# Listing one PSUM eviction further ahead in the hand-written order of a fused attention and feed-forward kernel

## Chip, cores and metric

The kernel runs on one core of a Trainium2 chip. The metric is the device time of one execution in microseconds (us). The kernel before took 239.92 us (median of 3 runs, 239.82 to 240.09).

## What is computed

Eight batches with eight heads, 576 tokens of 64 elements each, go through an attention without a score matrix: q gets a softmax over its 64 elements, k a softmax over the 576 tokens, and then k is multiplied with v first. The result, as 4608 rows of 512, goes through a gated feed-forward block with four weight matrices.

```python
def _attn_ref(q, k, v):                        # 8 x 8 x 576 x 64 each
    q_s = np.exp(q - max over the last axis);   q_s /= sum over the last axis + 1e-9
    k_s = np.exp(k - max over axis 2);          k_s /= sum over axis 2 + 1e-9
    kv = np.einsum('bhsd,bhse->bhde', k_s, v)
    return np.einsum('bhsd,bhde->bhse', q_s, kv)

def _moe_ref(x, w1, w2, w3, w_out):             # x 4608 x 512; 512x1024 twice, 1024x1024, 1024x512
    a = x @ w1
    b = x @ w2
    h = a * b @ w3
    return h @ w_out
```

(The four lines of the softmaxes are written shorter here than in the source.)

## The kernel before

The two weights behind the product are folded into one at the start (W3O = w3 times w_out). After that each batch b goes through an attention part and gives 576 rows of x. Of these, 512 are chunk b of the feed-forward block; the 64 that are left, the tail, are gathered over all eight batches in one tile xtail, and that is chunk 8, worked last. Everything that TensorE multiplies is in 16 bits.

The work is cut into named steps, and a step is written with its parts joined by points. Those that matter here:

- kmx.b, cba.b, cbx.b, cb.b, ksub.b, kexp.b: the maximum of k over the tokens. kmx (VectorE, line 501, two halves for later batches) reduces within the partitions, cba (VectorE) is a transposition of 32 x 32 blocks (line 517) and a reduction (line 520), cbx four small copies on ScalarE (line 528), cb one more reduction and transposition on VectorE (lines 534 and 536). ksub (line 578) subtracts it on GpSimd, and kexp is the exponential on ScalarE.
- kv.b: k times v on TensorE (line 603). kve.b adds the epsilon on ScalarE (line 620), and kv2.b divides on VectorE (lines 631 and 633).
- qn.b.p, qd.b.p: the last multiplication of q's softmax (GpSimd, line 677) and its transposition by a DMA on SP's queue (line 700).
- xm.b.h and xt.b: q times kv on TensorE (line 725), xm for the 512 rows of the chunk in two halves of two PSUM banks each, xt for the 64 rows of the tail, in two banks with 128 columns used. xs.b.h.i and xts.b.i scale them out of PSUM (ScalarE: line 339, VectorE: line 341), the first into x of the chunk, the second into xtail.
- up.1.c.s.u and up.0.c.s.u: chunk c times w2 and times w1 (line 857), four matmuls into one bank each. bs.c.s.u moves the first out of PSUM (line 335) on ScalarE or VectorE, and ab.c.s.u multiplies the second with it on VectorE (line 872).
- down.c.t: eight matmuls with W3O (line 879). os.c.t moves the result out (line 335), and st.c.t stores it by SP's queue (line 905).

PSUM is divided into pools: pab with four banks for the up products (and, from batch 3 on, for xt and half of xm), po with two banks for down (and for the other half of xm), att with two for the rest. A step that takes a bank waits until the step that empties it is done.

The order of the work is written out by hand: the long string ORDER lists all 793 steps, PICKS says which engine works each eviction and each elementwise step, and `Plan.run` emits the steps one after another in that order. Each engine works its own instructions in the order in which they were emitted; between engines there are only semaphores for data and for buffers. So the place of a step in ORDER decides what is in front of it on its own engine, and nothing else. An exception are steps added with the port flag: among the first 580 steps, `link` adds a wait between such steps when they change from GpSimd to VectorE or back. The evictions xs and xts carry no such flag, ksub, qsub and qn do.

xts.4.1 is the eviction of the second of the two banks of xt.4, the tail of chunk 4; PICKS gives it to VectorE. It stands in line 116 of the kernel before, behind cba.6 of the same engine. Behind it come down.3.1, down.3.2, kv2.5 and then up.1.4.0.0, the first product of chunk 4, which takes one of the pab banks. In line 833 the two xts steps are added:

```python
for i in range(2):
    A(("xts", b, i), moves(128), 0,
      lambda eng, i=i: xs(("xt", b), i, lambda: xtail[:, i::2, b * HALF:(b + 1) * HALF], eng),
      [("xt", b)], gives=[("xt", b)])
```

Of the kernel before, what the change touches and what calls it, by code (L numbers as in the profile page):

```python
# [17 lines left out]
class Plan:  # L18
# [93 lines left out]
os.2.1 down.2.2 down.2.3 cb.5 ksub.5.0 bs.3.0.5 qd.4.0 ab.3.0.5 qrc.5.1 ab.3.0.4 up.1.3.0.6  # L112
up.0.3.0.6 kv2.4 os.2.2 os.2.3 qmx.6.1 bs.3.0.6 xm.4.1 xt.3 qeps.5.0 ab.3.0.6 qrc.5.0 xs.4.1.1
ksub.5.1 kexp.5.0 qn.5.0 xs.4.1.0 qmx.6.0 k.6 up.1.3.0.7 bs.3.0.7 up.0.3.0.7 ab.3.0.7 down.3.0
kmx.6.0 os.3.0 kmx.6.1 kexp.5.1 xts.3.0 xts.3.1 xm.4.0 xt.4 kv.5 kve.5 xs.4.0.0 xts.4.0 xs.4.0.1
qn.5.1 cba.6 xts.4.1 down.3.1 down.3.2 kv2.5 up.1.4.0.0 vc.6.0 bs.4.0.0 cbx.6 st.2.2 up.0.4.0.0
up.1.4.0.1 up.0.4.0.1 up.1.4.0.2 qd.5.0 st.2.1 qd.5.1 st.2.3 ab.4.0.0 qsub.6.1 bs.4.0.1 st.3.0 q.7
k.7 v.7 os.3.1 os.3.2 st.3.1 ab.4.0.1 cb.6 xm.5.1 xm.5.0 bs.4.0.2 xs.5.0.1 xs.5.0.0 xs.5.1.1
qexp.6.1 ksub.6.1 up.0.4.0.2 up.1.4.0.3 qsub.6.0 ab.4.0.2 up.0.4.0.3 up.1.4.0.4 bs.4.0.3 up.0.4.0.4
# [881 lines left out]
```

## Time and profile before

| | |
|---|---|
| median of 3 runs | 239.92 us |
| the profiled execution | 240.03 us |
| its span, first to last instruction | 238.2 us |
| mean granted TensorE clock | 0.999 |
| TensorE busy (matmul) | 229.9 us, 97% of the span |
| VectorE busy | 172.9 us, 73% |
| ScalarE busy | 122.0 us, 51% |
| GpSimd busy | 115.5 us, 48% |
| moved by DMA | 46.84 MB, 197 GB/s over the span |

In the profile PE is TensorE, PEld its weight loads, DVE is VectorE, ACT is ScalarE, POOL is GpSimd and SPq the queue of SyncE, which issues most of the transfers. Times are microseconds from the start of the span. A row of the timeline gives the start, the time taken, the engine, the line of the kernel, the operation and its operands with the number of instructions that were merged, and in brackets the idle time in front of it with what ended it. A row of the waits gives the engine and line that waited, for what, the total, the number of times and the longest. Buffer numbers are left out of names, so xt, xm and the up products all appear as pab or po.

### The profile page before, as it was taken

Reading aid. Unit: us, or ns where it says so; the run is one execution under the profiler, and the core shown is the slowest. Engines: PE = TensorE matmul, PEld = TensorE weight load, DVE = VectorE, ACT = ScalarE, POOL = GpSimd, SP = SyncE. Lnnn points to the kernel's source line nnn. Section 1 sums busy time; section 2 is a strip of 40 time slices with the busy share of each in tenths; the row PEclk is TensorE's granted clock in tenths of the full one; section 3 lists DMA queues with packets and bytes.
Section 4 is the critical chain, followed back from the end, with each engine's and each line's share of the span. In section 5 each row is a group of like instructions: output and inputs, shape, how many; then the busy total and the mean of one; then the engine's idle time right before and its main releaser. Section 6 shows DMA issues by size and latency. Waiting matters only on the chain.

```text
span 238.2 us, 4852 instructions
## 1 busy us (share of the span) xinstructions
PE 229.9 (97%) x1935; PEld 119.2 (50%) x1935; DVE 172.9 (73%) x263; ACT 122.0 (51%) x225; POOL 115.5 (48%) x75
## 2 busy tenths in 40 slices
PE   7698999999999999999999999999999999999994
PEld 2445658865857444444443444444544444444443
DVE  2758699989889998999997799589554443444430
ACT  1442766498757867798754856574315011103021
POOL 8467168679939998596980938340500000000000
PEclk9999999999999999999999999999999999999999
DMA  6999999999999999998688945640630005144253
GB/s 208 214 307 209 342 202 303 321 306 385 296 218 300 402 359 273 390 384 151 237 115 210 398 153 101 132 89 3 106 84 0 0 4 131 25 96 94 53 132 132
DMA packets 40038, 46.84 MB, mean 197 GB/s; under 512 B 18384, under 2 KB 24272, under 8 KB 40016
## 3 DMA queue, kind: packets, MB, share of 16 engines
q1 hardware_dynamic: 32480, 34.81, 52.0%
q0 software_dynamic: 7536, 11.73, 21.2%
q8 instruction: 15, 0.25, 0.4%
q14 instruction: 7, 0.06, 0.1%
HBM read 38.80 MB, written 9.44 MB: 202 GB/s over the span
## 4 chain that ended last, share of the span: by engine, by line
PE 86%; DMA 6%; DVE 5%; POOL 1%; issue 1%; ACT 0%; DVEq 0%; ACTq 0%; POOLq 0%
PE pab L857 52%; PE po L879 21%; DMA k<-in_k_dram 6%; PE po L469 4%; PE po L894 3%; PE pkv L603 2%; DVE km L501 2%; PE xm L725 1%; PE w3t L457 1%; PE pab L725 1%; DVE ab L872 1%; DVE kmx L510 1%; PE po L725 0%; POOL wosb L416 0%; POOL w L416 0%
## 5 line engine op out<-in xcount | busy, mean ns | idle before, releaser
L872 DVE TENSOR_TENSOR ab<-pab,bsb 128x512 f16<-128x512 f32 x72 | 48.4, 682 | 30.5 <-PE pab L857 15.8
L857 PE MATMUL pab<-x,w2sb 128*128 128x512 f16 (+1 forms) x320 | 66.0, 337 | 0.6 <-DVE xtail L341 0.6
L857 PE MATMUL pab<-x,w1sb 128*128 128x512 f16 (+1 forms) x320 | 65.9, 337 | 0.0
L879 PE MATMUL po<-W3O,ab 128*128 128x512 f16 x256 | 59.2, 379 | 0.0
L857 PEld LDWEIGHTS <-w1sb 128*128 128x128 f16 x352 | 34.1, 98 | 28.4 <-issue 0.8
L857 PEld LDWEIGHTS <-w2sb 128*128 128x128 f16 x352 | 33.5, 98 | 29.0 <-DVE xtail L341 1.1
L335 ACT CAST bsb<-pab 128x512 f16<-128x512 f32 x47 | 27.1, 585 | 27.8 <-PE pab L857 27.4
L578 POOL TENSOR_TENSOR k<-k,cb 128x1152 f32<-128x1152 f32 x12 | 31.5, 2632 | 20.2 <-issue 10.8
L677 POOL TENSOR_TENSOR en<-eq,qr 128x1280 f16<-128x1280 f16 (+1 forms) x15 | 32.8, 2193 | 17.0 <-ACT qr L664 10.0
L879 PEld LDWEIGHTS <-ab 128*128 128x128 f16 x256 | 24.5, 98 | 29.0 <-issue 0.4
L335 ACT COPY osb<-po 128x512 f32<-128x512 f32 (+1 forms) x26 | 14.8, 575 | 40.9 <-PE po L879 35.4
L645 POOL TENSOR_TENSOR q<-q,qm 128x1024 f32<-128x1024 f32 (+1 forms) x14 | 29.7, 2124 | 5.8 <-issue 4.1
L640 DVE TENSOR_REDUCE qm<-q 128x16 f32<-128x1024 f32 (+1 forms) x16 | 21.4, 1340 | 3.5 <-DMA q<-in_q_dram 3.5
L658 DVE TENSOR_REDUCE qr<-eq 128x20 f32<-128x1280 f16 (+1 forms) x16 | 21.4, 1336 | 1.7 <-ACT eq L653 1.7
L335 DVE CAST bsb<-pab 128x512 f16<-128x512 f32 x25 | 17.1, 683 | 7.5 <-PE pab L857 6.9
L586 ACT ACTIVATE ek<-k 128x1152 f16<-128x1152 f32 x16 | 18.6, 1163 | 6.8 <-DVE k L578 3.6
L653 ACT ACTIVATE eq<-q 128x1024 f16<-128x1024 f32 (+1 forms) x16 | 18.5, 1163 | 3.9 <-DVE q L645 3.0
L501 DVE TENSOR_REDUCE km<-k 128x128 f32<-128x1152 f32 x8 | 17.3, 2166 | 0.0
L469 PE MATMUL po<-wosb,w3T 128*128 128x512 f16 x64 | 15.5, 379 | 0.7 <-DMA wosb<-in_moe_w_out_dram 0.5
L335 DVE COPY osb<-po 128x512 f32<-128x512 f32 (+1 forms) x11 | 7.2, 664 | 5.9 <-PE po L894 5.6
L335 ACT CAST v<-v 128x1152 f16<-128x1152 f32 x9 | 10.3, 1159 | 1.9 <-DMA v<-in_v_dram 1.9
L469 PEld LDWEIGHTS <-w3T 128*128 128x128 f16 x64 | 5.8, 98 | 7.3 <-issue 1.0
(78 smaller groups left out, 190.7 us busy)
## 6 DMA issues: line engine op xcount, KB each, us to landing
out_dram<-osb SPq DMA_DIRECT2D x64, 128.0 KB, 2.4
q<-in_q_dram SPq DMA_DIRECT2D x6, 1152.0 KB, 7.9
v<-in_v_dram SPq DMA_DIRECT2D x5, 1152.0 KB, 9.1
k<-in_k_dram SPq DMA_DIRECT2D x4, 1152.0 KB, 8.8
k<-in_k_dram POOLq DMA_DIRECT2D x3, 1152.0 KB, 13.6
v<-in_v_dram POOLq DMA_DIRECT2D x1, 1152.0 KB, 12.0
k<-in_k_dram SPq DMA_DIRECT2D x2, 576.0 KB, 7.6
v<-in_v_dram SPq DMA_DIRECT2D x2, 576.0 KB, 9.5
```

Of the source, the lines that this page charges most:

```text
L335: return [(nc.scalar.copy if eng == "ACT" else engine[eng].tensor_copy)(out=out, in_=in_)]
L469: nc.tensor.matmul(st["pf", ft], lhsT=st["w3T", ft][:, gt, :], rhs=wosb[:, gt, :], start=(gt == 0), stop=(gt == N_FT - 1))
L501: dve.tensor_reduce(out=st["km", b][:, two(hp), :], in_=kb[:, two(hp), :, :].rearrange("p h j d -> p h d j"), axis=AX.X, op=ALU.max)
L578: return [engine[eng].tensor_tensor(out=kb[:, two(hp), :, :], in0=kb[:, two(hp), :, :], in1=st["cb", b][:, two(hp), None, :].broadcast_to( ...
L586: nc.scalar.activation(out=st["ek", b][:, hp, :, :].rearrange("p j (i d) -> p i j d", i=2), in_=kb[:, two(hp), :, :], func=AF.Exp)
L640: dve.tensor_reduce(out=st["qm", b][:, :, j], in_=qb[:, :, j, :], axis=AX.X, op=ALU.max)
L645: return [engine[eng].tensor_tensor(out=qb[:, :, j, :], in0=qb[:, :, j, :], in1=st["qm", b][:, :, j, None].broadcast_to([P, HH, n, D]), op ...
L658: dve.tensor_reduce(out=st["qr", b][:, :, slice(*PARTS[p])], in_=st["eq", b, p], axis=AX.X, op=ALU.add)
L677: return [engine[eng].tensor_tensor(out=st["en", b][:, j, :, :].rearrange("p j h d -> p h j d"), in0=st["eq", b, p], in1=st["qr", b][:, :, ...
L857: nc.tensor.matmul(st["p", one, c, sub, u][:, a * (t1 - t0):(a + 1) * (t1 - t0)], lhsT=w[:, ct, fb * P:(fb + 1) * P], rhs=x()[:, ct, t0:t1 ...
L872: dve.tensor_tensor(out=st["ab", c][:, nf * u:nf * u + nf, t0:t1], in0=cut(st["p", 0, c, sub, u]), in1=cut(st["bsb", c, sub, u]), op=ALU.mult)
L879: nc.tensor.matmul(st["po", c, tb], lhsT=st["ab", c][:, ft, tb * P:(tb + 1) * P], rhs=W3O[:, ft, :], start=(ft == 0), stop=(ft == N_FT - 1))
```

## The change

The name xts.4.1 moves in ORDER from behind cba.6 to directly behind xt.4, the step whose result it takes out of PSUM. The seven steps between (kv.5, kve.5, xs.4.0.0, xts.4.0, xs.4.0.1, qn.5.1 and cba.6) are listed after it instead, in the order that they had. The engine stays VectorE; in PICKS only the place of the entry changes.

```diff
@@ -112,8 +112,8 @@
-kmx.6.0 os.3.0 kmx.6.1 kexp.5.1 xts.3.0 xts.3.1 xm.4.0 xt.4 kv.5 kve.5 xs.4.0.0 xts.4.0 xs.4.0.1
-qn.5.1 cba.6 xts.4.1 down.3.1 down.3.2 kv2.5 up.1.4.0.0 vc.6.0 bs.4.0.0 cbx.6 st.2.2 up.0.4.0.0
+kmx.6.0 os.3.0 kmx.6.1 kexp.5.1 xts.3.0 xts.3.1 xm.4.0 xt.4 xts.4.1 kv.5 kve.5 xs.4.0.0 xts.4.0
+xs.4.0.1 qn.5.1 cba.6 down.3.1 down.3.2 kv2.5 up.1.4.0.0 vc.6.0 bs.4.0.0 cbx.6 st.2.2 up.0.4.0.0
```

4 rows, old and new, of the table PICKS are left out of this document.

## The prediction

> **What bounds the kernel now.** I read the page first: busy time by engine, the shares of the chain that ended last, and the groups of instructions with the idle time in front of them.
>
> ```profile
> span 238.2 us, 4852 instructions
> ...
> PE 229.9 (97%) x1935; PEld 119.2 (50%) x1935; DVE 172.9 (73%) x263; ACT 122.0 (51%) x225; POOL 115.5 (48%) x75
> ...
> PE 86%; DMA 6%; DVE 5%; POOL 1%; issue 1%; ACT 0%; DVEq 0%; ACTq 0%; POOLq 0%
> ...
> L857 PE MATMUL pab<-x,w2sb 128*128 128x512 f16 (+1 forms) x320 | 66.0, 337 | 0.6 <-DVE xtail L341 0.6
> ```
>
> TensorE is busy for 97% of the span and carries 86% of the last chain, so the kernel is paced by TensorE, and what can be won is the time in which it stands still. The last row names one such place: a matmul of the first product stood 0.6 us behind an eviction into xtail on VectorE. The view of TensorE's waits lists all of them:
>
> ```profile
> PE w3t L457 <- DMA w<-in_moe_w_dram: 2.4, 3, 1.3
> PE po L362 <- DVE zero L357: 1.6, 1, 1.6
> PE pab L857 <- DVE xtail L341: 0.6, 1, 0.6
> PE po L469 <- DMA wosb<-in_moe_w_out_dram: 0.5, 1, 0.5
> PE po L469 <- DVE w3T L335: 0.2, 1, 0.2
> ```
>
> Four of the five rows belong to the weights and constants at the start. Only the third lies inside the pipeline, and it is the step that the change moves. The chain of waits shows it too: the eviction ends it on VectorE, and from 125.62 it runs on TensorE up to the last eviction (the pieces left out are all TensorE's until 235.25).
>
> ```profile
> 124.95 0.42 DVE mx L520
> 125.37 0.21 DVE xtail L341
> 125.58 0.05 issue
> 125.62 4.49 PE pab L857 x20
> ...
> 235.31 0.32 ACT osb L335
> ```
>
> **The stall in detail.** Here is the timeline around it, VectorE first, then TensorE and its weight loads (PEld), then ScalarE.
>
> ```profile
> 122.25 2.19 DVE L501 TENSOR_REDUCE km<-k 128x128 f32<-128x1152 f32 x1
> 124.47 0.45 DVE L517 STREAM_TRANSPOSE kmq<-km 128x256 f32<-128x256 f32 x1
> 124.95 0.42 DVE L520 TENSOR_REDUCE mx<-kmq 128x8 f32<-128x256 f32 x1
> 125.28 0.28 DVE L341 TENSOR_SCALAR xtail<-pab 128x128 f16<-128x128 f32 x1
> 125.48 0.17 DVE L631 RECIPROCAL rc<-rc 128x4 f32<-128x4 f32 x1
> ...
> 120.34 0.47 PE L725 MATMUL pab<-qT,kv 64*64 64x512 f16 x12
> 124.18 0.81 PE L879 MATMUL po<-W3O,ab 128*128 128x512 f16 x3
> 125.62 0.55 PEld L857 LDWEIGHTS <-w2sb 128*128 128x128 f16 x4 [1.13 <-DVE xtail L341]
> 125.62 1.04 PE L857 MATMUL pab<-x,w2sb 128*128 128x512 f16 x4 [0.64 <-DVE xtail L341]
> 126.50 1.03 PE L857 MATMUL pab<-x,w1sb 128*128 128x512 f16 x4
> 127.36 1.03 PE L857 MATMUL pab<-x,w2sb 128*128 128x512 f16 x4
> ...
> 122.55 0.62 ACT L339 ACTIVATE x<-pab 128x512 f16<-128x512 f32 x1
> ...
> L879 PE MATMUL po<-W3O,ab x18: 379/379/389, 119.8 to 124.6; 128*128 128x512 f16 x18
> ```
>
> The waiting instruction is the first weight load of up.1.4.0.0. Its PSUM bank is the one that xt.4 filled for its second half, and xts.4.1 must empty it first. The three L879 rows end at 124.18 + 0.81 = 124.99; one matmul takes 0.379, so the last of them started at 124.61, which is the 124.6 of the last row. Between 126.50 and 127.36 lie four matmuls, so they start 0.215 apart when nothing holds them, though each is shown for 0.379. The next matmul could have started at 124.61 + 0.215 = 124.82 and started at 125.62. **The stall is therefore 0.80 us**, not the 0.64 that the row prints, which counts from the modelled end of the matmul before.
>
> **The change part by part.** On VectorE xts.4.1 passes two instructions, the transposition of 0.45 and the reduction of 0.42 (both are cba.6). The other steps that it passes, kv.5 on TensorE, kve.5, xs.4.0.0, xts.4.0 and xs.4.0.1 on ScalarE, and qn.5.1 on GpSimd, lie on other engines, whose built orders stay as they were. It issues no transfer and passes no step of SP's queue, and it takes no part in the hand-made chain between VectorE and GpSimd, since its step is added without the port flag. The bank that up.1.4.0.0 takes stays the same, and its weight load still waits for xts.4.1, now at a VectorE count that is lower by two.
>
> Its input has long been there: xt.4's matmuls are among the twelve L725 rows and ended by 120.34 + 0.47 = 120.81. So it starts as soon as the reduction before it lets go. That reduction ends at 122.25 + 2.19 = 124.44. In the old order xts.4.1 started at 125.28, while the reduction in front of it is shown to 124.95 + 0.42 = 125.37, an overlap of 0.09. The pair below shows as much behind the very kind of reduction that it will now follow:
>
> ```profile
> 146.40 2.09 DVE L501 TENSOR_REDUCE km<-k 128x128 f32<-128x1152 f32 x1
> 148.40 0.68 DVE L872 TENSOR_TENSOR ab<-pab,bsb 128x512 f16<-128x512 f32 x1
> ```
>
> The reduction there ends at 148.49, the next one starts at 148.40, so 0.09. I take a start at 124.44 - 0.09 = 124.35, an end at 124.35 + 0.28 = 124.63, and a release after the same 0.06 as before (125.28 + 0.28 = 125.56 against 125.62): the weight load can go at 124.69. The weight load itself takes 0.098:
>
> ```profile
> L857 PEld LDWEIGHTS <-w2sb 128*128 128x128 f16 x352 | 33.5, 98 | 29.0 <-DVE xtail L341 1.1
> ```
>
> So the matmul is ready at 124.79, and TensorE itself is free at 124.82. The stall goes whole: **-0.80 us**, from 125.62 to 124.82, and no more than that, since the matmul before is then the limit. Only 0.03 is to spare: each 0.1 by which the eviction comes later than 124.35 costs some 0.07 to 0.1 of the gain.
>
> [...]
>
> What else could hold that first matmul? It reads the x of chunk 4, whose last part ScalarE wrote at 122.55 + 0.62 = 123.17, well ahead of 124.82. Nothing else is late there.
>
> The two instructions of cba.6 go back by at most 0.28. Who needs them is ScalarE's four small copies, and behind those cb.6 and GpSimd's subtraction:
>
> ```profile
> 126.70 0.58 ACT L335 CAST bsb<-pab 128x512 f16<-128x512 f32 x1 [2.49 <-PE pab L857]
> 127.31 0.82 ACT L528 COPY mx<-mx 32x8 f32<-32x8 f32 x4
> 130.80 2.63 POOL L578 TENSOR_TENSOR k<-k,cb 128x1152 f32<-128x1152 f32 x1 [6.45 <-issue]
> ```
>
> The copies stand behind bs.4.0.0, which itself waits for TensorE; with TensorE 0.80 earlier they come at 126.51, and cba.6 ends at 125.37 + 0.28 = 125.65 at the latest. A cover of 0.86 remains, so I cost this at nothing. The reciprocal and kv2.5 behind do not move, as the three instructions ahead of them keep their sum.
>
> **Does 0.80 reach the end?** From 125.62 on no row of TensorE's waits is left, so it arrives by its own pace; what matters is whether what it meets there is late by then. The nearest meeting is xm.5.1, which needs the two po banks that os.3.1 and os.3.2 empty; a later one is ScalarE's cast of v.7, which waits for a transfer that does not move.
>
> ```profile
> 127.63 0.69 DVE L872 TENSOR_TENSOR ab<-pab,bsb 128x512 f16<-128x512 f32 x1 [1.39 <-PE pab L857]
> 128.24 1.28 DVE L335 COPY osb<-po 128x512 f32<-128x512 f32 x2
> 130.04 0.41 PE L725 MATMUL po<-qT,kv 64*64 64x512 f16 x4
> ...
> 139.93 1.16 ACT L335 CAST v<-v 128x1152 f16<-128x1152 f32 x1
> 142.90 0.59 ACT L335 COPY osb<-po 128x512 f32<-128x512 f32 x1 [1.81 <-PE po L879]
> ```
>
> The two copies end at 128.24 + 1.28 = 129.52, and xm.5.1 would now come at 130.04 - 0.80 = 129.24. But the copies follow ab.4.0.0, which had stood idle 1.39 for TensorE, so they move ahead by 0.80 as well, to 128.72. The cast of v.7 cannot start earlier than its data; ScalarE then idles 1.81 for TensorE, so 0.80 less still leaves 1.01. VectorE, GpSimd and ScalarE in between are released by TensorE's chunk 4 products in the same way, and move with it.
>
> **The sum.** The profiled execution took 240.03 (span 238.2 and 1.83 around it); 240.03 - 0.80 = 239.23. It lies 0.11 above the median of the runs, 239.92, so as a median I forecast **239.12**, or 0.33% less. A measurement of this kernel can tell about 0.2%, or 0.48, from no change: the borders are 239.44 and 240.40.
>
> **The rivals.** [...] Against it are the two overlaps; 6%. (2) TensorE gains 0.80 and meets the po banks not yet empty, since os.3.1 and os.3.2 are held by their output buffers or something else that does not move. If they end at 129.52 as before, xm.5.1's second bank is free at 129.58, 0.34 after its new time; 0.46 is left, a median of 239.46. For it speaks that of TensorE's meetings this is the closest that I see; against it the idle 1.39 before ab.4.0.0. 10%. (3) Slower: the k chain. cba.6 ends 0.28 later, and if ScalarE's copies, cb.6 and GpSimd's subtraction at 130.80 pass that on, the exponentials and bs casts behind them on ScalarE come 0.28 later, then VectorE, and TensorE waits. The copies also stand in front of bs.4.0.1 and bs.4.0.2 on ScalarE. That decides from the point where the slip outlasts the cover of 0.86; a slip of 0.28 does not, unless the copies have to wait for something else of cba.6. If all 0.28 passed and nothing of the gain were left, 239.92 + 0.28 = 240.20; if it held up both evictions one after the other, 239.92 + 0.56 = 240.48. 4%, half for each. (4) The change does nothing: the pool hands up.1.4.0.0 a bank that is freed as late as before, or VectorE's order stays. The built order speaks against it; 239.92, 3%.
>
> **How the numbers follow.** The forecast keeps 77%. The range runs from 238.92 (0.80 gained, and 0.2 for the runs, which lay from 239.82 to 240.09) to 239.60, which takes in the first two rivals with 0.14 above the second; it holds nine in ten by these cases, and I leave some of that for what I have not seen. Faster by over 0.2% are the forecast and the first rival, 83%; within 0.2% are the second, the fourth and half of the third, 15%; slower by over 0.2%, 2%.
>
> **What would show it.** In the profile after: xts.4.1 at about 124.35 in front of the transposition; no row of TensorE's waits with xtail; the first L857 matmul of chunk 4 at about 124.82; and every later TensorE row, xm.5.1 at 129.24 for one, 0.80 earlier, up to a span of 237.4. The forecast is wrong if the L857 row still waits after 124.9, or if a new wait stands in front of xm.5.1 or later.

## The result: 239.31 us against 239.93

The changed kernel took 239.31 us (median of 21 runs, 238.97 to 239.71), the kernel before 239.93 on the same chip (21 runs, 239.77 to 240.14): a ratio of 0.9975, with a 95% interval of 0.9968 to 0.9982. It is faster by 0.62, or 0.26%. The profiled execution after took 239.15, with a span of 237.4; the profiled execution before had 240.03 and 238.2.

First the page of the kernel after: the span, the busy times, the shares of the chain that ended last, and the group of first products, whose last column is the idle time in front of it. Then all of TensorE's waits.

```profile
span 237.4 us, 4852 instructions
...
PE 229.5 (97%) x1935; PEld 119.1 (50%) x1935; DVE 172.7 (73%) x263; ACT 122.1 (51%) x225; POOL 115.5 (49%) x75
...
PE 90%; DMA 6%; DVE 1%; POOL 1%; issue 1%; ACT 0%; ACTq 0%; DVEq 0%; POOLq 0%
...
L857 PE MATMUL pab<-x,w2sb 128*128 128x512 f16 (+1 forms) x320 | 66.0, 337 | 0.0
```

```profile
PE w3t L457 <- DMA w<-in_moe_w_dram: 2.5, 3, 1.4
PE po L362 <- DVE zero L357: 1.6, 1, 1.6
PE po L469 <- DMA wosb<-in_moe_w_out_dram: 0.5, 1, 0.5
PE po L469 <- DVE w3T L335: 0.2, 1, 0.2
```

The idle time in front of the first products went from 0.6 to 0.0. The wait for xtail is gone, the four others are those of the start, and no new one has come. VectorE's share of the last chain fell from 5% to 1%: the chain used to lead back from the stalled product into VectorE, and now stays on TensorE. TensorE's own busy time is about as before (229.5 against 229.9), as it should be: no work was taken away.

The timeline of the kernel after around the place, VectorE first, then TensorE with its weight loads, then ScalarE:

```profile
122.21 2.18 DVE L501 TENSOR_REDUCE km<-k 128x128 f32<-128x1152 f32 x1
124.30 0.29 DVE L341 TENSOR_SCALAR xtail<-pab 128x128 f16<-128x128 f32 x1
124.49 0.44 DVE L517 STREAM_TRANSPOSE kmq<-km 128x256 f32<-128x256 f32 x1
124.97 0.42 DVE L520 TENSOR_REDUCE mx<-kmq 128x8 f32<-128x256 f32 x1
125.31 0.17 DVE L631 RECIPROCAL rc<-rc 128x4 f32<-128x4 f32 x1
...
121.31 3.63 PE L879 MATMUL po<-W3O,ab 128*128 128x512 f16 x16
124.64 0.67 PEld L857 LDWEIGHTS <-w2sb 128*128 128x128 f16 x4 [0.19 <-DVE xtail L341]
124.78 1.03 PE L857 MATMUL pab<-x,w2sb 128*128 128x512 f16 x4
129.19 0.41 PE L725 MATMUL po<-qT,kv 64*64 64x512 f16 x4
...
126.45 0.82 ACT L528 COPY mx<-mx 32x8 f32<-32x8 f32 x4
```

The eviction into xtail now stands between the long reduction and the transposition, and its shown time overlaps both: it starts 0.09 ahead of the reduction's end, and the transposition starts 0.10 ahead of the eviction's (124.49 against 124.30 + 0.29 = 124.59). So it puts the transposition off by little: 124.49 against 124.47, in an execution that is 0.05 ahead here. The first weight load of chunk 4 still waits for it, by 0.19, but the matmul does not: its row has no bracket, and it starts at 124.78, one interval behind the last matmul of down.3.2. Followed matmul by matmul through the two traces, every start from 73.3 (xm.2.0) up to the last matmul of down.3.2 lies 0.05 earlier than before, and every start from the first product of chunk 4 to the end of the kernel lies 0.84 to 0.86 earlier. The step between the two, 0.80, is the stall. Ahead of 73.3 the two executions differ by other amounts, from the weights at the start on, so the 0.05 is a difference between executions and not of the change.

### The profile page after: what moved, and what is told of

Its sections match the earlier page's. It is cut to its first block, busy times and chain, and to the rows that moved or that the text cites. A ratio compares the mean times of both kernels' runs of the same rounds, so it can differ in the third digit from the quotient of the medians.

```text
span 237.4 us, 4852 instructions
## 1 busy us (share of the span) xinstructions
PE 229.5 (97%) x1935; PEld 119.1 (50%) x1935; DVE 172.7 (73%) x263; ACT 122.1 (51%) x225; POOL 115.5 (49%) x75
## 4 chain that ended last, share of the span: by engine, by line
PE 90%; DMA 6%; DVE 1%; POOL 1%; issue 1%; ACT 0%; ACTq 0%; DVEq 0%; POOLq 0%
PE pab L857 53%; PE po L879 24%; DMA k<-in_k_dram 6%; PE po L469 4%; PE po L894 3%; PE pkv L603 2%; PE xm L725 1%; PE pab L725 1%; PE w3t L457 1%; PE po L725 1%; DVE kmx L510 1%; POOL wosb L416 0%; POOL w L416 0%; DVE kmx L511 0%; DVE w3T L335 0%
```

## The experiments

Two theories stood against one another. **A, the release:** the first product of chunk 4 waits for its PSUM bank; what counts is only when that bank is emptied, and by which engine does not matter. **B, VectorE's sequence:** what counts is the order and the length of VectorE's own work at this place, and the bank only shows it. A variant of A, called A1 below, adds that executions differ from one another only in what lies ahead of chunk 4, and that the old stall absorbed late arrivals of TensorE; A2, against it, has a wait behind 125 that holds up some executions.

For each run I took two numbers from its trace, matmul by matmul: the start of the last matmul of down.3.2 (the arrival) and that of the first product of chunk 4. The stall is their difference less 0.2155, the spacing of matmuls that nothing holds up. The last column is the time from that first product to the end of the last matmul.

| run | arrival | first product | stall | from there to the end |
|---|---|---|---|---|
| before | 124.609 | 125.623 | 0.80 | 109.61 |
| after | 124.563 | 124.779 | 0.00 | 109.60 |
| e1_half | 124.696 | 125.217 | 0.31 | 109.61 |
| e2_late | 124.728 | 124.944 | 0.00 | 109.60 |
| e3_act | 124.776 | 124.992 | 0.00 | 109.60 |
| e4_again (the change) | 124.599 | 124.814 | 0.00 | 109.60 |
| e5_dummy_after | 124.821 | 125.037 | 0.00 | 109.60 |
| e6_dummy_before | 125.067 | 125.283 | 0.00 | 109.60 |
| e7_third (the change) | 124.759 | 124.975 | 0.00 | 109.60 |
| e8_fourth (the change) | 124.799 | 125.015 | 0.00 | 109.60 |
| e9_store_after | 124.530 | 124.746 | 0.00 | 109.60 |
| e10_store_before | 124.531 | 125.546 | 0.80 | 109.61 |
| e11_after_side (the change) | 124.738 | 124.954 | 0.00 | 109.60 |
| e12_store_side | 124.592 | 124.808 | 0.00 | 109.60 |

**e1_half: half of the move.** cba.6 is split (cbr.6 is its reduction, line 520), and xts.4.1 stands between its two instructions.

```diff
-qn.5.1 cba.6 xts.4.1 down.3.1 down.3.2 kv2.5 up.1.4.0.0 vc.6.0 bs.4.0.0 cbx.6 st.2.2 up.0.4.0.0
+qn.5.1 cba.6 xts.4.1 cbr.6 down.3.1 down.3.2 kv2.5 up.1.4.0.0 vc.6.0 bs.4.0.0 cbx.6 st.2.2 up.0.4.0.0
```

> xts.4.1 stands between the two instructions of cba.6, behind the transposition and ahead of the reduction. Theory A (the gain is the earlier release of the PSUM bank, and nothing else): the eviction starts about 0.09 ahead of the transposition's end, at 124.84, and ends at 125.12, TensorE starts chunk 4 at about 125.18 instead of 125.62; the stall shrinks from 0.80 to 0.36, so 0.44 us faster than before, some 239.5, and slower than the whole change. Theory B (the gain comes from VectorE's own sequence, in which the eviction fills a gap between two dependent instructions, so that kv2.5 comes 0.17 us earlier): the gap is filled here too, so as fast as the whole change, 239.3.

It took 239.78 (11 runs) against 240.07 of the kernel before (20 runs), a ratio of 0.9985 (0.9976 to 0.9994). VectorE, the weight load and TensorE in its timeline:

```profile
124.54 0.45 DVE L517 STREAM_TRANSPOSE kmq<-km 128x256 f32<-128x256 f32 x1
124.91 0.25 DVE L341 TENSOR_SCALAR xtail<-pab 128x128 f16<-128x128 f32 x1
125.08 0.40 DVE L520 TENSOR_REDUCE mx<-kmq 128x8 f32<-128x256 f32 x1
125.21 0.55 PEld L857 LDWEIGHTS <-w2sb 128*128 128x128 f16 x4 [0.63 <-DVE xtail L341]
125.22 1.04 PE L857 MATMUL pab<-x,w2sb 128*128 128x512 f16 x4
```

The release comes at 124.91 + 0.25 = 125.16, the weight load 0.05 later and the product with it. A part of the stall is left, 0.31, so 0.49 of 0.80 is won in the trace; the medians show 0.29, and the interval (0.14 to 0.58) holds both. The stall follows the moment of release, as A has it; B, which expected the time of the whole change, missed.

**e2_late: the eviction even later than before.** It is moved in the other direction, behind kv2.5.

```diff
-qn.5.1 cba.6 xts.4.1 down.3.1 down.3.2 kv2.5 up.1.4.0.0 vc.6.0 bs.4.0.0 cbx.6 st.2.2 up.0.4.0.0
+qn.5.1 cba.6 down.3.1 down.3.2 kv2.5 xts.4.1 up.1.4.0.0 vc.6.0 bs.4.0.0 cbx.6 st.2.2 up.0.4.0.0
```

> xts.4.1 stands behind kv2.5 on VectorE, later than in the kernel before by the reciprocal and the two multiplications. Theory A: the eviction starts at about 125.88, TensorE's first weight load of chunk 4 goes at 126.22, 0.60 later than before, a stall of 1.40; 0.60 slower than before if the end of the kernel follows TensorE one to one, some 240.5. Theory B: VectorE's sequence is as long as before, and kv2.5 even comes 0.2 earlier, so the same time as before or a little faster, 239.7 to 239.9.

A was wrong here, and so was B: 239.25 (6 runs), a ratio of 0.9969 (0.9957 to 0.9980), as good as the change itself, where A expected 240.5 and B 239.7 to 239.9.

```profile
121.48 3.63 PE L879 MATMUL po<-W3O,ab 128*128 128x512 f16 x16
124.73 0.75 PEld L857 LDWEIGHTS <-w2sb 128*128 128x128 f16 x4
124.94 1.03 PE L857 MATMUL pab<-x,w2sb 128*128 128x512 f16 x4
126.06 0.28 DVE L341 TENSOR_SCALAR xtail<-pab 128x128 f16<-128x128 f32 x1
```

The eviction starts at 126.06, over a microsecond behind the product that used to wait for it. The built programs tell why: the pool handed the products other banks.

| kernel | banks of the first four products of chunk 4 (3 is the bank that xts.4.1 empties) |
|---|---|
| before, after, e1_half | 3, 1, 2, 0 |
| e2_late, e6_dummy_before | 1, 2, 3, 0 |
| e3_act | 1, 2, 0, 3 |

In e2_late the first product takes bank 1, which ScalarE empties with x of chunk 4 by 122.64 (its eviction starts at 122.04 and takes 0.60), and bank 3 goes to the third product. The traces agree: in e2_late and e6_dummy_before the third product, and no longer the first, carries the wait for VectorE's semaphore; its first weight load goes at 126.46 in e2_late, behind the eviction's end at 126.06 + 0.28 = 126.34, and at 126.80 in e6_dummy_before, behind 126.26 + 0.23 = 126.49. So A needs an addition: when the bank is emptied decides, and also which bank it is. And a step's place in ORDER does not only decide what stands in front of it on its own engine, as the description of the kernel before has it; it can also change which banks later steps are given. That the pool chooses by when it expects each bank to be empty is what the three rows suggest; how it reckons was not tried. In the changed kernel the banks are those of the kernel before, so the change itself gained by the earlier release alone.

**e3_act: the same place, another engine.** ScalarE does the eviction.

```diff
-    "qn_5_1": "POOL", "xts_4_1": "DVE", "vc_6_0": "ACT", "bs_4_0_0": "ACT", "qsub_6_1": "POOL",
+    "qn_5_1": "POOL", "xts_4_1": "ACT", "vc_6_0": "ACT", "bs_4_0_0": "ACT", "qsub_6_1": "POOL",
```

> xts.4.1 at its old place in the list, but on ScalarE, where it runs right behind xs.4.0.1 at about 123.1, some 1.2 us ahead of the eviction in the changed kernel. Theory A: the bank is free long before TensorE wants it, so the stall is gone, 0.6 to 0.8 faster than before and no faster than the whole change, since TensorE's matmul before is then the limit; 239.1 to 239.4. Theory B: VectorE has one instruction of 0.28 less, so kv2.5 comes still earlier and the time falls below that of the change, 239.0 or less.

239.34 (9 runs), a ratio of 0.9974 (0.9964 to 0.9983).

```profile
123.18 0.31 ACT L339 ACTIVATE xtail<-pab 128x128 f16<-128x128 f32 x1
124.99 1.03 PE L857 MATMUL pab<-x,w2sb 128*128 128x512 f16 x4
```

The eviction is through 1.5 ahead of the product, and VectorE is rid of it; still nothing beyond the change is won. Since the bank changed too, this run does not tell the moment of release from the choice of bank; it does tell that 0.80 is all that there was. B, with 239.0 or less, missed again.

**e4_again: the changed kernel beside these three.**

> The changed kernel itself once more, for a second trace of it, because its 21 times lie between 238.97 and 239.71, twice as far apart as those of before. Theory A1 (the stall of 0.80 us also absorbed late arrivals of TensorE from the stages ahead; without it they go through to the end): an execution that takes longer than 239.15 has TensorE later in all rows from before 124 us on, and no new wait behind 125. Theory A2 (something behind 125 us that does not move with TensorE, the transfer of v.7 or an output buffer, now holds it up in some executions): the rows up to 125 agree within 0.1, and a new wait stands in a row behind it.

239.23 (5 runs) against 240.07, a ratio of 0.9966 (0.9954 to 0.9979). The gain here, on chip 14, is 0.84, not 0.62 (the chip of the result is not on record). In its trace no wait stands behind 125.

**e5_dummy_after and e6_dummy_before: an idle instruction on VectorE.** A memset of a tile that nobody reads is added behind cba.6, once in the changed kernel (where it delays only what follows), once in the kernel before (where it stands between cba.6 and xts.4.1).

```diff
-xs.4.0.1 qn.5.1 cba.6 down.3.1 down.3.2 kv2.5 up.1.4.0.0 vc.6.0 bs.4.0.0 cbx.6 st.2.2 up.0.4.0.0
+xs.4.0.1 qn.5.1 cba.6 dly down.3.1 down.3.2 kv2.5 up.1.4.0.0 vc.6.0 bs.4.0.0 cbx.6 st.2.2 up.0.4.0.0
...
+    plan.add(("dly",), "DVE", 0.5, lambda: dve.memset(dly, 0.0))
```

That is e5. In e6 the line of the kernel before is changed, and the same step is added:

```diff
-qn.5.1 cba.6 xts.4.1 down.3.1 down.3.2 kv2.5 up.1.4.0.0 vc.6.0 bs.4.0.0 cbx.6 st.2.2 up.0.4.0.0
+qn.5.1 cba.6 dly xts.4.1 down.3.1 down.3.2 kv2.5 up.1.4.0.0 vc.6.0 bs.4.0.0 cbx.6 st.2.2 up.0.4.0.0
```

> The changed kernel with an additional memset of an unused tile (128 x 512 in 32 bits, about 0.54 us by the 0.272 that half as much takes at the start) on VectorE behind cba.6. Theory A (only the release of the bank of xts.4.1 matters): the eviction is already done, so the time stays that of the changed kernel, 239.2 to 239.4; kv2.5 comes 0.54 later but is wanted only at about 129.2. Theory B (VectorE's sequence sets the time): 0.5 slower than the changed kernel, 239.8.

> The kernel before with the same additional memset on VectorE between cba.6 and xts.4.1, so the eviction ends 0.54 later, at about 126.1. In this build the pool gives up.1.4.0.0 another bank, the first one of xm.4.0, which ScalarE empties at about 122.5, and the bank of xts.4.1 goes to the third product, up.1.4.0.1, wanted at about 126.5. Theory A with the bank (TensorE waits for the eviction of whatever bank it is given): no stall at 124.8, and the time of the changed kernel, 239.2 to 239.4, in spite of more work in front of the eviction. Theory A without it (the place of the eviction on VectorE alone decides): 0.54 slower than before, 240.5. Theory B: 240.4.

e5 took 239.26 (8 runs), a ratio of 0.9962 (0.9949 to 0.9976) to 240.11 of the kernel before (17 runs). Its memset, and the next multiplication on VectorE:

```profile
125.70 0.48 DVE L960 MEMSET dly<- 128x512 f32 x1
127.03 0.69 DVE L872 TENSOR_TENSOR ab<-pab,bsb 128x512 f16<-128x512 f32 x1 [0.22 <-PE pab L857]
```

VectorE is 0.48 later and still waits 0.22 for TensorE: an idle VectorE hides it, and B falls. In e6, the kernel before with the memset in front of the eviction, the rows are

```profile
124.90 0.45 DVE L517 STREAM_TRANSPOSE kmq<-km 128x256 f32<-128x256 f32 x1
125.28 1.03 PE L857 MATMUL pab<-x,w2sb 128*128 128x512 f16 x4
125.38 0.42 DVE L520 TENSOR_REDUCE mx<-kmq 128x8 f32<-128x256 f32 x1
125.86 0.48 DVE L960 MEMSET dly<- 128x512 f32 x1
126.26 0.23 DVE L341 TENSOR_SCALAR xtail<-pab 128x128 f16<-128x128 f32 x1
```

It took 239.39 (9 runs), a ratio of 0.9966 (0.9956 to 0.9976). An instruction that does nothing, and delays the eviction to 126.26, makes the kernel before faster by 0.72, since the pool then hands out bank 1 first. This is the plainest sign that the choice of bank alone can make this stall or remove it.

**e7_third and e8_fourth: the changed kernel on chip 12, that of e5 and e6**, for its spread from execution to execution.

> The changed kernel once more, for another trace and more times. Theory A1 (differences between executions come from the stages ahead of 124 us): the span from the first matmul of chunk 4 to the end is within 0.05 of that in the two traces of this kernel so far, and what differs is where that matmul starts. Theory A2 (a wait behind 125 us in some executions): that stretch is longer in a slower execution.

> As the run before: one more trace of the changed kernel, to have a slower or a faster execution among the traces. Theory A1: only the start of chunk 4 differs. Theory A2: the stretch behind it differs.

e7 took 239.27 (5 runs) against 240.11, a ratio of 0.9960 (0.9944 to 0.9975), so again 0.84; e8, a single run, 239.39. In the table above the two arrive 0.20 and 0.24 later than the first trace of the same kernel, and from the first product on they take the same 109.60. A2 falls, and of A1 one half holds: executions differ ahead of chunk 4. The other half, that the old stall absorbed late arrivals, is not shown.

**e9 to e12: a store out of the way of a transposition.** A place ahead of chunk 4 where TensorE waits in some executions and not in others is xm.2.0, which needs q of batch 2, transposed by a DMA of SyncE's queue (qd.2.0). In that queue two stores of results stand in front of it (their four issues run from 63.57 to 66.69 in the kernel after, and the two transpositions of batch 2 are issued from 66.80 on). TensorE in e6_dummy_before and in the kernel after:

```profile
72.61 0.71 PE L857 MATMUL pab<-x,w1sb 128*128 128x256 f16 x5
73.63 0.41 PE L725 MATMUL xm<-qT,kv 64*64 64x512 f16 x4 [0.31 <-DMA qT<-en]
```

```profile
72.54 0.71 PE L857 MATMUL pab<-x,w1sb 128*128 128x256 f16 x5
73.31 0.41 PE L725 MATMUL xm<-qT,kv 64*64 64x512 f16 x4
```

So the store st.0.1 was listed behind qd.2.0, in the changed kernel (e9, on chip 7) and in the kernel before (e10, there too), and then the changed kernel with and without it side by side on chip 4 (e11 without, e12 with).

```diff
-st.0.1 qrc.2.1 qn.2.1 qsm.2.0 qd.2.1 vc.2.1 qeps.2.0 up.1.1.0.2 up.0.1.0.2 up.1.1.0.3 up.0.1.0.3
-qrc.2.0 qn.2.0 qd.2.0 bs.1.0.2 ab.1.0.2 bs.1.0.3 kv.2 kve.2 ab.1.0.3 down.1.0 kv2.2 qmx.3.1 xm.1.1
+qrc.2.1 qn.2.1 qsm.2.0 qd.2.1 vc.2.1 qeps.2.0 up.1.1.0.2 up.0.1.0.2 up.1.1.0.3 up.0.1.0.3
+qrc.2.0 qn.2.0 qd.2.0 st.0.1 bs.1.0.2 ab.1.0.2 bs.1.0.3 kv.2 kve.2 ab.1.0.3 down.1.0 kv2.2 qmx.3.1 xm.1.1
```

> The changed kernel with one more edit: the store of the second row of results of chunk 0 (st.0.1) is listed behind the transposition of q of batch 2 (qd.2.0) instead of six steps ahead of it, both on SyncE's queue. If the spread between executions comes from that transposition landing behind TensorE's own arrival at xm.2.0 (73.3 us): qd.2.0 is issued about 1.2 earlier (67.0 instead of 68.2), lands at about 72.0, xm.2.0 never waits (no row of its wait with qT), and the profiled start of the first product of chunk 4 lies at 124.7 or earlier; median 239.0 to 239.25, against about 239.27 of the changed kernel alone, so 0.0 to 0.3 faster. If the spread comes from elsewhere: the same 239.2 to 239.4 and the same scatter of the runs, 0.4 to 0.7 from the lowest to the highest. In both cases the stall in front of chunk 4 is 0.00, and from the first product of chunk 4 to the end of the last matmul TensorE takes 109.60.

> The kernel before with the same second edit (st.0.1 listed behind qd.2.0), the eviction at its old place. If the transposition sets the spread: 239.75 to 240.1, that is 0.0 to 0.3 below the kernel before, with the stall of 0.80 in front of chunk 4 unchanged or shorter where TensorE arrives no earlier; VectorE's reduction of k comes with its own inputs. An earlier arrival of TensorE at chunk 4 alone would be eaten by the stall, since xts.4.1 stands behind VectorE's work and not TensorE's: then the median stays at 240.0 and the stall grows by what TensorE came earlier. If neither matters: 239.9 to 240.1 and a stall of 0.80.

> The changed kernel as it is, on the same chip as its twin with the store moved (e12). If the move of the store matters for TensorE: 239.2 to 239.35 with a scatter of 0.4 or more, against 239.1 and a scatter of 0.2 of the twin. If it does not: both within 0.1 of one another, about 239.1 to 239.3, and the low scatter of the earlier five runs was chance. The kernel before with the store moved measured the same as the kernel before (240.01 against 240.00), which speaks for the second.

> The changed kernel with the store st.0.1 behind qd.2.0, again, beside the changed kernel on the same chip. If the move matters: 239.05 to 239.15, at least 0.1 below the twin, and the runs within 0.2 of one another. If it does not: within 0.1 of the twin and a scatter like the twin's. In both cases no stall in front of chunk 4, and 109.60 from its first product to the end of the last matmul.

| | median (runs) | lowest to highest | ratio to the kernel before |
|---|---|---|---|
| e9, the change and the store | 239.10 (5) | 238.95 to 239.15 | 0.9959 (0.9947 to 0.9972) |
| e10, the store alone | 240.01 (11) | 239.82 to 240.22 | 0.9999 (0.9990 to 1.0008) |
| e11, the change alone | 239.24 (5) | 239.01 to 239.31 | 0.9963 (0.9951 to 0.9976) |
| e12, the change and the store | 239.18 (5) | 239.05 to 239.25 | 0.9962 (0.9948 to 0.9975) |

TensorE in e9:

```profile
72.54 0.71 PE L857 MATMUL pab<-x,w1sb 128*128 128x256 f16 x5
73.18 0.41 PE L725 MATMUL xm<-qT,kv 64*64 64x512 f16 x4
```

With the store behind, the transpositions of batch 2 are issued from 65.52 on in e9, and xm.2.0 comes at 73.18, 0.13 earlier than in the kernel after, though the row in front of it starts at 72.54 in both; in e12 it comes at 73.20. From start to start across this place, seven of the eleven traces with the store at its old place lose 0.13 to 0.38, and the other four (before, e2_late, e4_again, e11_after_side) and the three with the store moved lose nothing. So the transposition is one source of the spread, and three traces are few to show that the move ends it. In the times the move is not to be told from nothing: 0.06 between e12 and e11, and e10 equals the kernel before. No version is shown to beat the changed kernel.

## Why the prediction was right, and where its number was off

- **The stall and its size.** Forecast: 0.80 and not the 0.64 of the row, and that it goes whole. Measured: 0.80 before, 0.00 after. This is the forecast's main step, and it held to the hundredth.
- **The times of the steps.** From 73.3 on, TensorE in this trace lies 0.05 earlier than in the one before, already ahead of the change. With that taken off, the forecasts of 124.35 for the eviction, 124.69 for the weight load, 124.82 for the product and 129.24 for xm.5.1 become 124.30, 124.64, 124.77 and 129.19; the rows show 124.30, 124.64, 124.78 and 129.19. The span came out at 237.4, as forecast.
- **The narrow margin.** Forecast: 0.03 to spare. Measured: the weight load goes at 124.64 and takes 0.098 by the prediction's row, so it is done at 124.74, 0.04 ahead of the matmul.
- **Rival 1 (6%), a pause of VectorE between two instructions.** No run shows such a pause in front of the eviction. In its place the rows show an overlap: the reduction ends at 122.21 + 2.18 = 124.39 and the eviction starts at 124.30, 0.09 ahead of that shown end, and in e1_half it starts at 124.91, 0.08 ahead of the transposition's (124.54 + 0.45 = 124.99).
- **Rivals 2 and 3.** xm.5.1 waits for nothing at 129.19, and ScalarE's copies come at 126.45, behind cba.6's end at 124.97 + 0.42 = 125.39. Neither cover was used up; e5_dummy_after put 0.48 more on VectorE at that place at no cost. One reading on the way was off, to the harmless side: the reciprocal was not to move, as the three instructions ahead of it keep their sum, but it came at 125.31, 0.17 earlier than before, 0.12 with the 0.05 taken off. The eviction overlaps both its neighbours now, and in the old order nothing overlapped the start of the transposition (124.47, behind a reduction that ends at 124.44).
- **Rival 4, another bank.** It did not happen in this change. The prediction named the pool's choice only as a way to gain nothing; e2_late and e6_dummy_before show that it is as strong a lever as the release here, and that it can win the same 0.80. That was missing from the reasoning.
- **From the trace to the median.** Here lies the 0.19 between 239.12 and 239.31. The forecast took the profiled 239.23 and subtracted 0.11, because that execution of the kernel before lay 0.11 above the median of three. The profiled run after, at 239.15, is 0.08 below the 239.23, of which 0.05 came ahead of the change; but it lies 0.16 below its own median, and the 21 runs span 0.74. So the mis-sized term is the correction from one execution to a median, not the stall. A single execution says little about where the median lies when the arrival at chunk 4 differs by up to 0.5 between traces (124.53 to 125.07 in the table).
- **What stays open.** The change won 0.62, 0.84, 0.84 and 0.75 in four measurements; the four intervals have 0.9968 to 0.9975 in common, that is 0.60 to 0.77 of 240.0, and the 0.80 of the traces, 0.9967, lies just outside the interval of the first. That a late TensorE eats part of the old stall would explain it, but the traces speak against it: the long reduction on VectorE starts 2.35 to 2.40 ahead of TensorE's arrival in all fourteen, so VectorE comes late together with TensorE. The two traces with the whole old stall, before and e10, are of early arrivals, though (124.61 and 124.53), so a late one was not seen with it. What sets the arrival from execution to execution is shown in part only. At 67.5 the matmuls of the fourteen traces lie within 0.21 of one another; the transposition of q at xm.2.0 adds up to 0.38 (e6_dummy_before: 73.63 - 72.61 = 1.02, against 73.18 - 72.54 = 0.64 in e9), and the products of k and v near 90 another 0.10 to 0.14 in five of them, whose cause stays open. e9 to e12 did not turn this into time.

## What to carry to other kernels

When the engine that paces a kernel stands in front of an eviction, measure the stall from start to start of its instructions, and forecast the whole of it if the eviction's input has long been there and nothing else is late behind (here 0.80 of 0.80 in the trace). Then ask two questions, not one: when the buffer is emptied, and which buffer the pool hands out; a small reorder (e2_late), or even an idle instruction (e6_dummy_before), changed the second here. And give a forecast for the median a margin as wide as the arrivals differ between executions (here 0.54, from 124.53 to 125.07 in fourteen traces), since the profile is one of them.

## What the runs showed that was not expected

- The choice of bank: with another bank for the first product, and the eviction later by 0.78 (e2_late, 126.06 against 125.28), or with an added idle instruction of 0.48 in front of it (e6_dummy_before), the kernel before lost the same stall and became faster by 0.82 and 0.72.
- The rest of the kernel is very regular: from the first product of chunk 4 to the end of the last matmul, fourteen executions, twelve of them on four chips on record, took 109.60 to 109.61. Their scatter, 0.5 in arrival, arises ahead of it.
- A weight load that waited 0.18 to 0.19 for a bank (after, e4_again, e5_dummy_after) cost the matmul nothing there, as it takes 0.098 and is otherwise issued 0.21 ahead (124.73 to 124.94 in e2_late).
